# Sixteen narrow transfers for the MLP's two scalars, instead of 32 columns in the rows of its weights

## The chip, the cores and the metric

The kernel runs on one core of a Trainium2 chip, as one launch. The metric is device time in microseconds (us), the median over runs; lower is better. Profiles come from the hardware profiler and hold one execution each.

## The reference

One decoding step for 8 sequences: an attention block with grouped heads over a cache of 4096 keys, multiplied by the gate that a small gated MLP makes from the same normalised input. All is float32.

```python
xn = _layernorm(x)                                   # x: 8 x 1 x 512
# A: 32 query heads of 128, 8 key/value heads, caches 8 x 8 x 4096 x 128 (k and v)
q = (xn @ wq)                                        # wq: 512 x 4096
p = softmax(q k^T * 128**-0.5);  s = (p v) @ wo      # wo: 4096 x 512
# B: the MLP
z  = gelu(xn @ w_in)                                 # w_in: 512 x 1792
z1 = z[..., :896];  z2 = layernorm(z[..., 896:])
g  = w_sp * z2 + b_sp                                # w_sp is 1 x 1, b_sp has 1 element
B  = (z1 * g) @ w_out                                # w_out: 896 x 512
return x + s * silu(B)
```

The two scalars `w_sp` and `b_sp` are what this case is about.

## The kernel before

The caches and weights are rearranged on the host, so that each of the three large buffers in the core's memory (`slot_a`, `slot_b`, `slot_c`, each 128 partitions x 16384 floats, 8 MB) is filled by one transfer with one contiguous row per partition. All large transfers are issued by one engine's queue, SP's. The MLP's weights come as one array `w_mlp` of 128 rows: 7168 floats of `w_in`, 3584 of `w_out`, and 32 more, `side`, of which the first two are `w_sp` and `b_sp`, the same in each row. It goes into `slot_c`, which the first half of the first head's values takes over once the MLP is done.

Two parts follow each other.

- `prologue` is written against a scheduling library, which keeps the instructions of SP in the order of the code here and sets the semaphores itself. It has eight semaphores for transfers from SP's queue (named `DMAHW0` to `DMAHW7`) and hands them out in turn, one to each transfer. SP issues `wq` into `slot_b`, `x`, `w_mlp` into `slot_c`, and the first half of head 0's keys (`k0`, "in_kT") into `slot_a`; that one has a semaphore of its own, `landed_a`. Then come layer norm, the queries (L151, TensorE), their place in `q`, the second half of the keys (`k1`) into `slot_b` as soon as the queries are done (L161), and the MLP: products L176, GELU, layer norm, `z2 * w_sp + b_sp` at L202 on VectorE, products L211, and the gate at L224.
- `Heads` is ordered by hand, with semaphores of its own. For each of 8 heads: products with the two halves of the keys (L362), softmax, products with the two halves of the values (L384). `loads` issues on SP the transfers of 8 MB in the order in which buffers come free: values first half into `slot_c`, second half into `slot_b`, the next head's keys into `slot_a` and `slot_b`. `wo` comes in 7 pieces behind the last values. The first of these transfers, values into `slot_c` (L275), stands behind the end of the prologue on all engines.

At L202 the scalars are read from `side_sb`, the last 32 columns of the MLP's rows:

```python
nc.vector.tensor_scalar(z2, z2, side_sb[:, 0:1], side_sb[:, 1:2], op0=ALU.mult, op1=ALU.add)
```

Of the kernel before, what the change touches and what calls it, by code (L numbers as in the profile page):

```python
# [10 lines left out]
P = 128  # L11
B, D = 8, 512
# [4 lines left out]
R = 32  # L17
FH = 896
FQ = 256
NB = FH // P  # L20
# [9 lines left out]
AHEAD = FOLDED + 2  # L30
HD = 256
N_IN, N_OUT = NK * 2 * FH, NB * D
N_MLP = N_IN + N_OUT + R
STEPS = 8
WARM = 384
AHEAD_OF_V = 11
# [52 lines left out]
        self.same_all = self.same.rearrange("p g r -> p (g r)")  # L89


def prologue(tc, t, x, w_mlp, wq, k0, k1, landed_a, landed_b):

    nc = tc.nc
    slot_a, slot_b, slot_c = t.slots
# [1 line left out]
    wq_sb = slot_b.rearrange("p (k n) -> p k n", k=NK)  # L97
    w_in_sb = slot_c[:, :N_IN].rearrange("p (k n) -> p k n", k=NK)
    w_out_sb = slot_c[:, N_IN:N_IN + N_OUT].rearrange("p (j d) -> p j d", j=NB)
    side_sb = slot_c[:, N_IN + N_OUT:N_MLP]  # L100
    x_sb = slot_c[:B, N_MLP + P:N_MLP + P + D]
    xn = slot_c[:B, N_MLP + P + D:N_MLP + P + 2 * D]
    nc.sync.dma_start(x_sb, x)
    nc.sync.dma_start(slot_c[:, :N_MLP], w_mlp)
    first = nc.sync.dma_start(slot_a, k0).then_inc(landed_a, 16)
    tc.no_tile_sem_insts.add(first.ins.name)

# [341 lines left out]
        step(mm)  # L449


def gqa_gmlp_decode(nc, x, kT, v, wq, wo, w_mlp, x_rows, out):
    t = Chip(nc)
    landed_a, landed_b, stored = (nc.alloc_semaphore(s) for s in ("landed_a", "landed_b", "stored"))
    with tile.TileContext(nc) as tc:
        prologue(tc, t, x, w_mlp, wq, kT[0, 0], kT[0, 1], landed_a, landed_b)
    heads = Heads(nc, t, landed_a, landed_b, stored)
    heads.loads(kT, v, wo, x_rows)
    for h in range(HKV):
        heads.head_sides(h)  # L460
    heads.last_sides(out)
    nc.sync.wait_ge(stored, 16).then_inc(stored, -16)
    with nc.tensor.Fori(0, HKV):
        heads.head_products()
    heads.last_products()
# [39 lines left out]
```

## Time and profile before

| | |
|---|---|
| median of 3 runs | 678.76 us (678.47 to 679.23) |
| span of the profiled execution, first to last instruction | 677.3 us |
| that execution's place beside the runs | its span is 1.46 us below the median of the runs' device times |
| instructions | 5977 |
| busy: TensorE, VectorE, ScalarE, GpSimd | 409.4, 80.8, 13.8, 2.8 us |
| transfers | 290.90 MB in 6214 packets, 429 GB/s on average |

The profile numbers lines as the kernel above. A transfer's row gives the time at which SP starts to issue it; "us to landing" counts from there to the last of its completions. "SPq" is SP's queue of instructions; a share of DMA time is a share of what the core's 16 DMA engines could be busy.

### The profile page before, as it was taken

The numbers are of one execution on the slowest core, as the hardware profiler recorded it, in microseconds if no ns is written. First come the engines' busy times: TensorE is split into PE (matmuls) and PEld (weight loads), VectorE is DVE, ScalarE is ACT, GpSimd is POOL, SyncE is SP. The second block draws the span as 40 slices with busy tenths as digits, with TensorE's granted clock in tenths as the row PEclk, the third lists the DMA queues.
The fourth block names the chain that finished last, engine by engine and source line by source line (L and its number), as shares of the span: only waits on it lengthen the run. The fifth ranks groups of instructions, "written<-read, shape, count | busy, mean of one in ns | idle before, by whom it ended". The sixth has DMA issues, their size and how long they took to land. (4 is left out here: it accounts for less than half of the span.)

```text
span 677.3 us, 5977 instructions
## 1 busy us (share of the span) xinstructions
PE 409.4 (60%) x2660; PEld 134.0 (20%) x2660; DVE 80.8 (12%) x156; ACT 13.8 (2%) x28; POOL 2.8 (0%) x15
## 2 busy tenths in 40 slices
PE   0456749446875449455794459555693349655598
PEld 0112213112221113111131113111131113211134
DVE  0142021102110021101110021101100021100211
ACT  0010000000000000000000000000000000000000
POOL 1000000000000000000000000000000000000000
PEclk9986859787896669787696779877696788976699
DMA  9999999999999999999999999999999999999997
GB/s 379 443 433 434 434 434 433 434 433 433 433 433 433 433 433 433 433 433 433 433 433 433 433 433 433 433 433 433 433 433 433 433 433 434 433 433 433 433 448 300
DMA packets 6214, 290.90 MB, mean 429 GB/s; under 512 B 952, under 2 KB 1080, under 8 KB 1600
## 3 DMA queue, kind: packets, MB, share of 16 engines
q1 hardware_dynamic: 6064, 290.79, 99.3%
q8 instruction: 4, 0.07, 0.0%
q10 hardware_dynamic: 144, 0.03, 0.0%
q14 instruction: 2, 0.02, 0.0%
HBM read 290.78 MB, written 0.03 MB: 429 GB/s over the span
## 5 line engine op out<-in xcount | busy, mean ns | idle before, releaser
L362 PE MATMUL sc<-slot_b,q 128*32 128x512 f32 x512 | 73.8, 741 | 74.8 <-PEq L344 74.8
L362 PE MATMUL sc<-slot_a,q 128*32 128x512 f32 x512 | 72.9, 733 | 72.0 <-PEq L344 72.0
L384 PE MATMUL o_ps<-slot_c,pT 128*16 128x512 f32 x512 | 73.6, 739 | 48.4 <-PEq L344 48.4
L377 PE MATMUL scr<-pT,ident 128*128 128x512 f32 x176 | 77.7, 597 | 0.0
L384 PE MATMUL o_ps<-slot_b,pT 128*16 128x512 f32 x512 | 56.5, 593 | 4.2 <-PEq L344 4.2
L362 PEld LDWEIGHTS sc<-slot_b,q 128*32 128x32 f32 x512 | 20.7, 133 | 127.9 <-issue 127.9
L261 DVE TENSOR_REDUCE nm<-sc 128x1 f32<-128x1024 f32 x8 | 9.8, 1225 | 290.7 <-PE sc L362 290.7
L362 PEld LDWEIGHTS sc<-slot_a,q 128*32 128x32 f32 x512 | 20.1, 131 | 118.4 <-issue 118.4
L377 PEld LDWEIGHTS scr<-pT,ident 128*128 128x128 f32 x176 | 32.8, 190 | 45.1 <-issue 45.1
L261 DVE TENSOR_TENSOR o_all<-o_ps,diag 128x512 f32<-128x512 f32 x16 | 11.1, 692 | 225.2 <-PE o_ps L384 225.2
L384 PEld LDWEIGHTS o_ps<-slot_c,pT 128*16 128x16 f32 x512 | 17.3, 113 | 98.1 <-issue 98.1
L384 PEld LDWEIGHTS o_ps<-slot_b,pT 128*16 128x16 f32 x512 | 15.6, 97 | 44.2 <-issue 44.2
L292 ACT ACTIVATE p<-sc,nm 128x1024 f32<-128x1024 f32 x8 | 8.9, 1115 | 554.1 <-DVE nm L261 554.1
L261 DVE TENSOR_REDUCE o_sb<-o_all 128x128 f32<-128x512 f32 x16 | 16.5, 1033 | 0.5
L143 PE MATMUL scr<-ident,slot_c 8*128 8x8 f32 x4 | 0.6, 254 | 25.1 <-DVE slot_c L140 25.1
L349 PE MATMUL scr<-pT,ident 128*128 128x384 f32 x36 | 13.8, 507 | 0.0
L151 PE MATMUL scr<-slot_b,xnT 128*32 128x512 f32 x64 | 10.2, 792 | 0.3 <-DVE xnT L144 0.3
L261 DVE STREAM_TRANSPOSE pT<-p 128x1024 f32<-128x1024 f32 x8 | 10.0, 1245 | 0.3
L366 PE MATMUL scr<-ident,nm 128*1 128x128 f32 x8 | 2.2, 269 | 11.9 <-PEq L344 11.9
L370 PE MATMUL scr<-wl,same 128*128 128x1 f32 x16 | 3.6, 297 | 6.6 <-PEq L344 6.6
L392 PE MATMUL po<-fold,o_sb 128*128 128x16 f32 x32 | 6.1, 266 | 2.5 <-PEq L344 2.5
L392 PEld LDWEIGHTS po<-fold,o_sb 128*128 128x128 f32 x32 | 4.8, 188 | 14.0 <-issue 14.0
(94 smaller groups left out, 91.2 us busy)
## 6 DMA issues: line engine op xcount, KB each, us to landing
slot_c<-in_w_mlp SPq DMA_DIRECT2D x1, 5392.0 KB, 34.0
slot_a<-in_wo SPq DMA_DIRECT2D x1, 4608.0 KB, 39.1
slot_a<-in_wo SPq DMA_DIRECT2D x1, 1280.0 KB, 41.7
slot_a<-in_wo SPq DMA_DIRECT2D x2, 512.0 KB, 44.2
slot_a<-in_wo SPq DMA_DIRECT2D x1, 768.0 KB, 43.1
slot_a<-in_wo SPq DMA_DIRECT2D x1, 384.0 KB, 45.1
slot_a<-in_kT SPq DMA_DIRECT2D x8, 48.5
slot_b<-in_kT SPq DMA_DIRECT2D x8, 31.4
```

The source lines that it names most:

```text
L143: nc.tensor.transpose(pt[:, k * B:(k + 1) * B], xn[:, k * P:(k + 1) * P], t.ident[:B, :B])
L151: nc.tensor.matmul(pq[R * g:R * (g + 1), :], t.xnT[:, k, :], wq_sb[:, k, lo:lo + REP * DH], start=(k == 0), stop=(k == NK - 1))
L261: make(*args, **kw).then_inc(self.dve, 1)
L292: nc.scalar.activation(p, t.sc.rearrange("p c s -> p (c s)"), AF.Exp, bias=t.nm, accum_out=t.l).then_inc(self.act, 1)
L349: self.nc.tensor.matmul(t.scr[1][:, :WARM], t.ident, t.pT.rearrange("p j b g r -> p (j b g r)")[:, :WARM], start=True, stop=True)
L362: mm = nc.tensor.matmul(t.sc[R * g:R * (g + 1), c, :], t.q[:, b * R:(b + 1) * R], k_sb[:, i, c, g, :], start=(b == 0), stop=(b == B - 1))
L366: step(nc.tensor.transpose(t.scr[0][:1, :P], t.nm, t.ident))
L370: step(nc.tensor.matmul(t.scr[1][:, 1:2], t.same_all, t.wl, start=True, stop=True))
L377: nc.tensor.matmul(t.scr[1], t.ident, flat[:, :512], start=True, stop=True)
L384: mm = nc.tensor.matmul(of[R * i:R * i + G * REP, :], pT[:, j, half * HALF + i], v_sb[:, i, j], start=(j == 0), stop=(j == J - 1))
L392: mm = nc.tensor.matmul(t.po[:, half * n:(half + 1) * n], t.o_sb[half], t.fold.rearrange("p i r -> p (i r)"), start=True, stop=True)
```

## The change

The 32 columns leave `w_mlp`, whose rows become 10752 floats long instead of 10784. They come as an array of their own, `side` (128 rows of 32 floats, 128 bytes), into the same columns of `slot_c` as before, in sixteen transfers behind `w_mlp` on SP's queue: of 1, 2, 3 and so on up to 15 rows, and a last of 8 rows, 128 rows in all. The transfer of `k0` follows them.

```diff
-N_MLP = N_IN + N_OUT + R
+N_MLP = N_IN + N_OUT
...
-def prologue(tc, t, x, w_mlp, wq, k0, k1, landed_a, landed_b):
+def prologue(tc, t, x, w_mlp, side, wq, k0, k1, landed_a, landed_b):
...
-    side_sb = slot_c[:, N_IN + N_OUT:N_MLP]
+    side_sb = slot_c[:, N_MLP:N_MLP + R]
     x_sb = slot_c[:B, N_MLP + P:N_MLP + P + D]
     xn = slot_c[:B, N_MLP + P + D:N_MLP + P + 2 * D]
     nc.sync.dma_start(x_sb, x)
     nc.sync.dma_start(slot_c[:, :N_MLP], w_mlp)
+    row = 0
+    for rows in (*range(1, 16), B):
+        nc.sync.dma_start(side_sb[row:row + rows], side[row:row + rows])
+        row += rows
     first = nc.sync.dma_start(slot_a, k0).then_inc(landed_a, 16)
...
-            w_out.transpose(1, 0, 2).reshape(P, NB * D),
-            side], axis=1),
+            w_out.transpose(1, 0, 2).reshape(P, NB * D)], axis=1),
+        "side": side,
```

The lines of the changed kernel behind this place have numbers higher by 4 (L105 is L109, L202 is L206). On SP's queue, at the start of the program, stood before (the brackets name the semaphores on which a row waits):

```order
L96 DMA slot_b<-in_wq 128x16384
L103 DMA slot_c<-in_x 8x512
L104 DMA slot_c<-in_w_mlp 128x10784
L105 DMA slot_a<-in_kT 128x16384
L161 DMA slot_b<-in_kT 128x16384 [waits DMAHW0_52,PE_52]
```

In the changed kernel, behind `wq`, `x` and `w_mlp` and the transfers of 1 to 4 rows, none of which waits, there stands:

```order
L107 DMA slot_c<-in_side 5x32
L107 DMA slot_c<-in_side 6x32 [waits DMAHW0_52]
L107 DMA slot_c<-in_side 7x32 [waits DMAHW1_52]
L107 DMA slot_c<-in_side 8x32 [waits DMAHW2_52]
L107 DMA slot_c<-in_side 9x32 [waits DMAHW3_52]
L107 DMA slot_c<-in_side 10x32 [waits DMAHW4_52]
L107 DMA slot_c<-in_side 11x32 [waits DMAHW5_52]
L107 DMA slot_c<-in_side 12x32 [waits DMAHW6_52]
L107 DMA slot_c<-in_side 13x32 [waits DMAHW7_52]
L107 DMA slot_c<-in_side 14x32 [waits DMAHW0_52]
L107 DMA slot_c<-in_side 15x32 [waits DMAHW1_52]
L107 DMA slot_c<-in_side 8x32 [waits DMAHW2_52]
```

The transfer of `k0` (L109) stands behind the last of these rows, still without a wait of its own. The eight semaphores are handed out in turn, so that of `wq` is 0, of `x` 1, of `w_mlp` 2, of the sides of 1 to 5 rows 3 to 7; from the side of 6 rows on each transfer shares its semaphore with the one that stands eight places ahead of it in this row of transfers, and waits for that one's landing.

On VectorE, in the MLP, stood before:

```order
L191 TENSOR_SCALAR var<-scr 128x1 [waits PE_52]
L201 TENSOR_SCALAR p<-p,rs 128x256 [waits Pool_52]
L202 TENSOR_SCALAR p<-p,slot_c 128x256 [waits DMAHW2_52,DVE_52]
L203 TENSOR_TENSOR p<-p 128x256 [waits DVE_52]
L207 COPY pT<-scr 128x128 [waits PE_52] x2
```

and now:

```order
L195 TENSOR_SCALAR var<-scr 128x1 [waits PE_52]
L205 TENSOR_SCALAR p<-p,rs 128x256 [waits Pool_52]
L206 TENSOR_SCALAR p<-p,slot_c 128x256 [waits DMAHW4_52,DMAHW3_52,DMAHW5_52,DMAHW2_52,DMAHW6_52,DMAHW1_52,DMAHW7_52,DMAHW0_52,DVE_52]
L207 TENSOR_TENSOR p<-p 128x256 [waits DVE_52]
L211 COPY pT<-scr 128x128 [waits PE_52] x2
```

The order on VectorE is the same; the operation that reads the scalars waits for all eight transfer semaphores instead of one.

More of the change, by code (lines that the diff above doesn't have):

```diff
@@ L449, in last_products, with gqa_gmlp_decode @@
         step(mm)
-def gqa_gmlp_decode(nc, x, kT, v, wq, wo, w_mlp, x_rows, out):
+def gqa_gmlp_decode(nc, x, kT, v, wq, wo, w_mlp, side, x_rows, out):
     t = Chip(nc)
@@ L455, in gqa_gmlp_decode @@
     with tile.TileContext(nc) as tc:
-        prologue(tc, t, x, w_mlp, wq, kT[0, 0], kT[0, 1], landed_a, landed_b)
+        prologue(tc, t, x, w_mlp, side, wq, kT[0, 0], kT[0, 1], landed_a, landed_b)
     heads = Heads(nc, t, landed_a, landed_b, stored)
```

## The prediction

> **What bounds the kernel now.** I read the page first, its slices and queues, then busy time by stretches, then SP's own instructions in order of time. The page:
>
> ```profile
> span 677.3 us, 5977 instructions
> DMA  9999999999999999999999999999999999999997
> q1 hardware_dynamic: 6064, 290.79, 99.3%
> PE acc L428 0%; DVE gate L261 0%
> ```
>
> The 16 DMA engines are busy in each of the 40 slices but the last; SP's queue (q1) takes 99.3% of their time. The chain that ended last shows only the tail. TensorE, at 60%, is not the bound. By stretches:
>
> ```profile
> core 0: us, PE busy (x) PEld busy (x) DVE busy (x) ACT busy (x) POOL busy (x), PEclk, DMA share, GB/s
> 0.00:80.00 80.00, 34.77 (x236) 11.44 (x240) 15.32 (x41) 2.17 (x3) 2.83 (x15) 0.87 0.99 423
> 80.00:160.00 80.00, 50.11 (x310) 16.17 (x306) 8.10 (x14) 1.41 (x3) 0.00 (x0) 0.79 1.00 433
> 560.00:640.00 80.00, 51.12 (x310) 16.11 (x306) 7.90 (x13) 1.41 (x3) 0.00 (x0) 0.78 1.00 433
> ```
>
> From 80 to 640 us (the first and last of seven such stretches shown) the DMA share is 1.00, at 433 GB/s. So the time is bytes over rate, and any time in which the DMA engines have nothing queued is added to the end, because no later stretch has idle time to take it back. The question is whether the change leaves the engines without work. SP's issues in order of time:
>
> ```profile
> 0.74 0.37 SPq L96 DMA_DIRECT2D slot_b<-in_wq  x1
> 1.17 0.37 SPq L103 DMA_DIRECT2D slot_c<-in_x  x1
> 1.58 0.35 SPq L104 DMA_DIRECT2D slot_c<-in_w_mlp  x1
> 1.98 0.71 SPq L105 DMA_DIRECT2D slot_a<-in_kT  x1
> 37.59 0.33 SPq L161 DMA_DIRECT2D slot_b<-in_kT  x1
> 62.71 0.33 SPq L275 DMA_DIRECT2D slot_c<-in_v  x1
> 84.33 0.33 SPq L277 DMA_DIRECT2D slot_b<-in_v  x1
> 84.71 0.42 SPq L280 DMA_DIRECT2D slot_a<-in_kT  x1
> ```
>
> and from issue to landing (last column, us):
>
> ```profile
> slot_c<-in_w_mlp SPq DMA_DIRECT2D x1, 5392.0 KB, 34.0
> slot_b<-in_wq SPq DMA_DIRECT2D x1, 22.1
> slot_a<-in_kT SPq DMA_DIRECT2D x1, 52.9
> slot_b<-in_kT SPq DMA_DIRECT2D x1, 37.8
> slot_c<-in_v SPq DMA_DIRECT2D x1, 32.0
> ```
>
> Added to the issue times these give the landings: wq 22.84, w_mlp 35.58, k0 54.88, k1 75.39, the first values 94.71. Before, k0 is in the queue from 1.98 us on, 33.6 us before w_mlp has landed, so the engines go from the one to the other without a pause.
>
> **The change, part by part.**
>
> *Waits on SP.* In the new order SP issues wq, x, w_mlp and the sides of 1 to 5 rows without a wait, by about 4 us. The side of 6 rows waits for wq (semaphore 0) and that of 7 for x: both pass at 22.9 us, as the one wait for wq that before shows:
>
> ```profile
> L161 SPq EVENT_SEMAPHORE  x1: 17/17/17, 22.9 to 22.9; - x1
> ```
>
> That is 0.06 us behind the landing at 22.84, and costs nothing, since w_mlp is still moving. The side of 8 rows waits for semaphore 2, that of w_mlp: it can be issued at 35.58 + 0.06 = 35.64 us, and everything behind it on SP waits with it, k0 above all. By then the engines are empty but for a few rows of 128 bytes. The sides of 9 to 13 rows wait for those of 1 to 5, which lie in the queue right behind w_mlp and land with it; 14 and 15 wait for those of 6 and 7, the same. So nine issues stand between w_mlp's landing and k0's issue.
>
> *The price of one issue.* At the program's start issues follow each other by 0.43, 0.41 and 0.40 us (1.17 - 0.74 and so on); the shortest pair is 84.71 - 84.33 = 0.38; the longest run of issues is that of wo:
>
> ```profile
> 627.02 3.28 SPq L282 DMA_DIRECT2D slot_a<-in_wo  x7
> 630.34 16.94 SPq L283 DMA_DIRECT2D x_out<-in_x_rows  x1
> ```
>
> 7 in 630.34 - 627.02 = 3.32 us, 0.47 each. I take 0.41, the distance behind x, which is the nearest in kind (8 rows, under the library's semaphores): 9 x 0.41 = 3.7 us, bounds 3.4 and 4.3. A narrow transfer that takes as long to issue as the 0.71 of k0 would make 6.8 with 0.05 between; I keep that for the range. Below 0.38 no row goes. k0 is issued at 35.64 + 3.7 = 39.34 us instead of 1.98.
>
> *The last wait.* The last side (8 rows) shares semaphore 2 with the side of 8 rows at 35.64 and is reached eight issues later, at 38.9. The nearest landing of a small transfer on idle engines is the output's:
>
> ```profile
> out<-gate ACTq DMA_DIRECT2D x1, 32.0 KB, 1.5
> q10 hardware_dynamic: 144, 0.03, 6.2%
> ```
>
> 1.5 us from issue gives 37.1, so that wait is over 1.8 us before it is reached. It would bind only if a small landing took over 3.3 us.
>
> *The restart.* k0 is then the only work. wq is the one 8 MB transfer that starts on idle engines: 22.1 us from issue to landing. So k0 lands at 39.34 + 22.1 = 61.44 instead of 54.88: 6.56 us late. The lower bound: 8 MB in a running stream take 94.71 - 75.39 = 19.32 us (values behind k1), and a small transfer's 1.5 us covers issue, first packet and completion, in which its 144 packets take little: 19.3 + 1.4 = 20.7, 1.4 less. The upper: k0's own issue took 0.71, wq's 0.37, so 0.34 more. I take wq's, an identical transfer on an idle queue.
>
> *Extra packets.* 128 rows of data and their completions, some 256 packets more. The output's row prices a small packet: 6.2% of 16 engines over the 2.4 us of that answer, by 144, is 16.5 ns. 256 of them are 4.2 us of one engine, 0.26 us if spread. Here the most crowded engine may get one row and one completion of each transfer, 32 packets, 0.53 us. Those of 1 to 7 rows stand behind w_mlp and those of 8 and more in the pause, all ahead of k0's first packet. Covered by the pause; without it they would cost 0.26 to 0.53. By the Trainium skill ("DMA: Bandwidth & Descriptors", on why a DMA increments its semaphore by 16), a transfer uses the largest number of engines up to 16 that divides its rows, the lowest-numbered ones; the first engine then gets all sixteen. No view here splits the engines; this only chooses 0.53 over 0.26.
>
> *w_mlp shorter.* 128 x 128 bytes, 0.016 of 290.79 MB: 0.04 us at 433 GB/s, nothing.
>
> *What is queued behind k0.* k1's issue waits for the queries (37.59) and now also behind k0: 39.8, still 21 us ahead of k0's landing at 61.4. Covered. k1 lands near 82. L206 waits for all eight semaphores; the last side is issued at 38.9 and landed by 40.5, against the row
>
> ```profile
> L202 DVEq EVENT_SEMAPHORE  x1: 21/21/21, 52.9 to 52.9; - x1
> 53.26 0.41 DVE L202 TENSOR_SCALAR p<-p,slot_c 128x256 f32<-128x256 f32 x1
> 62.98 8.51 PE L362 MATMUL sc<-slot_a,q 128*32 128x512 f32 x64 [2.65 <-PEq L344]
> 75.51 4.91 PE L362 MATMUL sc<-slot_b,q 128*32 128x512 f32 x28 [4.01 <-PEq L344]
> ```
>
> 12 us early. Seven more waits of 0.02 us make 0.15 us, and as many again on SP at the prologue's end: the first values' issue moves from 62.71 to about 63.0, while k1 is moving until 82: covered by 19 us. TensorE's first products start at about 63.2, behind the 61.4 at which k0 has landed, and end 8.5 us later, before k1's 82. So TensorE waits longer for k1, and nothing of that shows. All later issues wait for TensorE's products of data that land 6.6 us later, and move with them.
>
> The 16.94 us of the last issue (L283) show that SP can be held in an issue when much is queued; there seven pieces of wo had gone out just before. In the new start eight transfers are out by 4 us and ten at 23 us; if that held SP too, it would hold it before w_mlp's landing, for which it has to wait anyhow.
>
> **The sum.** 3.7 (nine issues) + 0.06 + 22.1 - (54.88 - 35.58) = 6.56 us, 0 elsewhere. Against the profiled execution: span 677.3 + 6.6 = 683.9. The median of the runs stands 1.46 us above that span, and I add to it: 678.76 + 6.6 = 685.4 us, 1.0% slower.
>
> **Rivals.** *SP is not held (not slower).* If k0's issue came before about 34.1 us (w_mlp's landing at 35.58 less the output's 1.5), the queue would never run dry, and only the packets remain: 678.76 + 0.26 to 0.53 = 679.0 to 679.3, within 0.2%. For it: all issues take 0.4 us, 16 of them are 6.6 us, far ahead of 34.1. Against it: the order, in which the side of 8 rows waits for w_mlp's semaphore, and the row at 22.9, where SP did stand 20 us for such a semaphore. It decides at that one wait. 4%.
>
> *Each narrow transfer waits for the one before.* Then each of nine costs an issue and a landing, 0.37 + 1.5 = 1.9 us, 17.1 instead of 3.7: 6.6 + 13.4 = 20 us, 698.8. Against it: the waits name semaphores eight transfers back. 3%. The same page of the Trainium skill puts about 2.0 us of fixed cost on a DMA (section on the anatomy of one DMA, for transfers issued by GpSimd) and advises merging small ones; by that figure in turn the nine would be 18 us; the trace's 1.5 agrees in kind, but only if they were not in flight together.
>
> *Issuing narrow transfers is dear.* At 0.76 each the nine take 6.8 us: 9.7 us, 688.4. For it: issues of 3, 7 or 11 rows appear nowhere in this trace, and 0.71 does once. 10%.
>
> *The engines restart warm.* 20.7 instead of 22.1, and 0.38 an issue: 4.9 us, 683.6. 15%, the lower edge of the forecast's own spread.
>
> **The chances.** Forecast 67% (685.0 to 686.3 by the bounds of its issues, 3.4 and 4.3, and 0.34 on k0), the rivals 4, 3, 10 and 15%, and 1% for a gain of which I see no mechanism. The time is the forecast's. The range takes in the warm restart and the dear issues, 683.2 to 688.4, and leaves out about 1 in 10 (the first two rivals, and a little at both edges). Below 0.2% (1.36 us) a measurement of this kernel tells nothing from no change. Slower by more: 0.95; within: 0.04; faster: 0.01.
>
> **What would show it.** In SP's rows: an issue at L107 near 22.9 and one near 35.6, then nine at steps of about 0.4, L109 near 39.3 (before 1.98) with some 22 us to landing instead of 52.9. In the slices: the third (34.2 to 51.3 us of the longer span) falls from 433 to near 300 GB/s, all others stay; q1 has 6320 packets, and its share falls by about 0.8 points. L206 starts within 0.3 us of 53.3, the first values' issue within 0.5 of 62.7. Wrong would be: k0 issued before 34 us, steps of 0.7 or more, an idle stretch further on, or a later stage that takes some of the 6.6 us back.

## The result and the profile after

The changed kernel takes 684.67 us (684.52 to 684.86, 4 runs), against 678.66 us for the kernel before on the same chip: 1.0089 times as long, 95% interval 1.0077 to 1.0101. That is 6.0 us slower; 6.6 was forecast. The span of the profiled execution went from 677.3 to 683.2 us. Of the four runs of a kernel further down (`k0` ahead of the narrow transfers) one took 850.0 us; the numbers there are those of the other three.

The page of the changed kernel: span, slices of the DMA, and SP's queue.

```profile
span 683.2 us, 5998 instructions
DMA  9979999999999999999999999999999999999997
GB/s 399 415 308 427 430 427 434 435 430 430 430 430 445 453 437 430 430 434 430 430 434 437 430 430 430 430 460 441 434 430 430 434 430 430 437 434 430 430 438 304
q1 hardware_dynamic: 6320, 290.79, 98.5%
```

One slice fell, the third (34 to 51 us), to 308 GB/s. The busy digits of all others are those of before, so nothing was lost later and nothing made good. Of 16 engines' span SP's queue has 98.5% instead of 99.3. Around the hole, busy time by short stretches (the last two columns are the DMA share and GB/s):

```profile
33.00:35.00 2.00, 2.00 (x22) 0.68 (x24) 0.47 (x2) 0.00 (x0) 0.00 (x0) 1.00 0.57 238
35.00:36.00 1.00, 1.00 (x12) 0.26 (x8) 0.00 (x0) 0.00 (x0) 0.00 (x0) 1.00 0.00 0
36.00:38.00 2.00, 1.19 (x12) 0.42 (x4) 1.05 (x2) 0.00 (x0) 0.00 (x0) 1.00 0.03 3
38.00:40.00 2.00, 1.99 (x24) 0.76 (x26) 0.41 (x2) 0.00 (x0) 0.00 (x0) 1.00 0.43 134
```

From 35 to 38 us the DMA engines move 0 to 3 GB/s. SP's issues in order of time say why; the second answer begins at 35 us and so shows the last nine narrow transfers alone:

```profile
1.60 0.35 SPq L104 DMA_DIRECT2D slot_c<-in_w_mlp  x1
1.99 36.86 SPq L107 DMA_DIRECT2D slot_c<-in_side  x16
35.54 3.31 SPq L107 DMA_DIRECT2D slot_c<-in_side  x9
38.89 0.35 SPq L109 DMA_DIRECT2D slot_a<-in_kT  x1
39.28 0.43 SPq L165 DMA_DIRECT2D slot_b<-in_kT  x1
```

and the waits of SP's queue name what held it (total, times, longest, us):

```profile
SPq L107 <- DMA slot_b<-in_wq: 19.3, 1, 19.3
SPq L107 <- DMA slot_c<-in_w_mlp: 12.0, 1, 12.0
```

SP stood until 22.9 us for wq, which cost nothing, and until 35.54 for w_mlp. Then came nine issues in 3.35 us, and only then k0, at 38.89 us instead of 1.98. Time from issue to landing of k0 and k1:

```profile
DMA to landing us min/median/max: 23.1/23.1/23.1
DMA to landing us min/median/max: 42.0/42.0/42.0
```

k0 lands at 38.89 + 23.1 = 62.0 us (before 54.88) and k1 at 39.28 + 42.0 = 81.3 (before 75.39), 5.9 us late: the loss of the whole kernel is complete by then.

### The profile page after: what moved, and what is told of

It is laid out like the page before. It is cut to its first block, busy times and chain, and to the rows that moved or that the text cites. A ratio compares the mean times of both kernels' runs of the same rounds, so it can differ in the third digit from the quotient of the medians.

```text
span 683.2 us, 5998 instructions
## 1 busy us (share of the span) xinstructions
PE 408.5 (60%) x2660; PEld 133.3 (20%) x2660; DVE 80.8 (12%) x156; ACT 13.8 (2%) x28; POOL 2.8 (0%) x15
## 3 DMA queue, kind: packets, MB, share of 16 engines
q1 hardware_dynamic: 6320, 290.79, 98.5%
```

## The experiments

Three accounts were set against each other. *The held queue*: the transfers share eight semaphores, so that SP waits for w_mlp's landing ahead of k0's issue, and the engines run empty. *The small packets*: the 256 packets more cost the time. *Issues ahead of k0*: sixteen issues stand ahead of it, whatever they wait for.

**Seven and eight transfers.**

```diff
-    for rows in (*range(1, 16), B):
+    for rows in (1, 2, 3, 4, 3, 3, 112):       # seven
+    for rows in (1, 2, 3, 3, 2, 2, 3, 112):    # eight, in another kernel
```

For seven was expected:

> The 128 rows in seven transfers on SP's queue, of 1, 2, 3, 4, 3, 3 and 112 rows: the last still has a wait, but for x, none for w_mlp. If SP's wait for w_mlp's landing makes the loss (the held queue): k0 is issued at about 23.6 us, w_mlp is still moving until 35, no pause, 678.7 to 679.0 us. If the small packets make it (256 of them for 6.0 us): 160 packets here, +3.8, 682.4. If it is only that issues stand ahead of k0, whatever they wait for (sixteen for 6.0 us): seven, +2.6, 681.3.

For eight:

> The same rows in eight transfers, of 1, 2, 3, 3, 2, 2, 3 and 112 rows; 160 packets as with seven. The held queue: the eighth waits for w_mlp's landing, SP goes on at 35.5 and issues k0 after one transfer, at 35.95 instead of the 38.89 of the changed kernel, 2.9 us less loss: 681.7 us, 3.0 above seven transfers, with a pause of some 2 us in the DMA. The small packets: 682.4, the same as seven. Issues ahead of k0 alone: 0.4 above seven.

Measured: seven 678.49 us, a ratio of 0.9999 (0.9990 to 1.0009) to the kernel before; eight 681.62, 1.0045 (1.0028 to 1.0062). One transfer more, with the same number of packets, costs 3.1 us. SP's issues with seven:

```profile
1.97 21.46 SPq L107 DMA_DIRECT2D slot_c<-in_side  x7
23.48 0.43 SPq L109 DMA_DIRECT2D slot_a<-in_kT  x1
```

and with eight (from 35 us on):

```profile
35.48 0.32 SPq L107 DMA_DIRECT2D slot_c<-in_side  x1
35.84 0.44 SPq L109 DMA_DIRECT2D slot_a<-in_kT  x1
```

and from its waits:

```profile
SPq L107 <- DMA slot_c<-in_w_mlp: 12.1, 1, 12.1
```

With seven, SP is held as well, until 22.8 us and for wq; k0 is issued 12 us before w_mlp has landed, and nothing is lost. With eight the last transfer takes w_mlp's semaphore, k0 comes at 35.84, and the engines run empty. Packets alone and issues alone are out: neither can make a step of 3 us between seven and eight.

**Thirty-two transfers of 4 rows.** `for rows in (4,) * 32:`

> The change with 32 transfers of 4 rows: 25 of them stand between w_mlp's landing and k0's issue, instead of 9. The held queue, at the 0.27 us that the issue of 4 rows took in the changed kernel and 0.04 between: 25 x 0.31 = 7.7 us, k0 at 43.2 us, 4.3 later than in the changed kernel, 689.0 us. At the prediction's 0.41 an issue: 10.3 us, 691.6. The small packets: 256 of them as in the change, 684.7.

Measured: 689.49 us, 1.0163 (1.0146 to 1.0180). From 35 us on:

```profile
35.37 8.36 SPq L107 DMA_DIRECT2D slot_c<-in_side  x25
43.77 0.35 SPq L109 DMA_DIRECT2D slot_a<-in_kT  x1
```

25 issues in 8.4 us, 0.336 each; k0 at 43.77. The loss follows the issues that stand behind the wait.

**k0 ahead of the narrow transfers.**

```diff
+    first = nc.sync.dma_start(slot_a, k0).then_inc(landed_a, 16)
+    tc.no_tile_sem_insts.add(first.ins.name)
     row = 0
     for rows in (*range(1, 16), B):
...
-    first = nc.sync.dma_start(slot_a, k0).then_inc(landed_a, 16)
-    tc.no_tile_sem_insts.add(first.ins.name)
```

> k0 is issued ahead of the sixteen transfers, at 1.98 us as before the change. The held queue: the pause does not go but moves. The sides of 1 to 5 rows now land behind k0 (54.5 us), the side of 9 rows waits for that of 1, and k1 stands behind eight more issues, 3.0 us, at about 57.5 instead of 37.6; the DMA is empty from 54.5 on. The loss is the changed kernel's 6.0 less one issue of 0.32: 684.3 us. Issues ahead of k0 alone: 678.7. The small packets: 684.7, with no pause.

Measured: 684.16 us, 1.0083 (1.0063 to 1.0103): hardly better than the change itself. SP's issues from 54 us on:

```profile
54.50 2.97 SPq L109 DMA_DIRECT2D slot_c<-in_side  x8
57.52 0.35 SPq L165 DMA_DIRECT2D slot_b<-in_kT  x1
```

and from its waits:

```profile
SPq L109 <- DMA slot_c<-in_side: 18.9, 1, 18.9
```

The pause moved one transfer further: the sides now land behind k0, and k1 is the one that stands behind them, issued at 57.52 instead of 37.59.

**What a pause costs.** Four kernels have a pause behind a wait of SP's; the delay is the issue of the next 8 MB less the moment at which SP goes on:

| | SP goes on | next 8 MB issued | delay | loss against before | rest |
|---|---|---|---|---|---|
| eight transfers | 35.48 | 35.84 | 0.36 | 3.07 | 2.71 |
| k0 first | 54.50 | 57.52 | 3.02 | 5.61 | 2.59 |
| the change | 35.54 | 38.89 | 3.35 | 6.01 | 2.66 |
| thirty-two | 35.37 | 43.77 | 8.40 | 10.97 | 2.57 |

The loss is the delay plus 2.6 to 2.7 us, over a range of 0.4 to 8.4 us. So once the queue is left to run dry, it costs 2.6 us before a single extra issue is counted. The trace's packet records show what these are in the changed kernel. The first 64 KB packets of k0, one on each engine, start at 34.76 us on average in the kernel before. SP goes on only at 35.54, 0.78 later; the packets start 1.20 us behind k0's issue, at 40.09; and they take 3.12 us on average instead of 2.42, as those of wq at the program's start do (3.11). 0.78 + 1.20 + 0.70 = 2.68 us.

**The same sixteen from ScalarE's queue.** `nc.scalar.dma_start(...)` in place of `nc.sync.dma_start(...)` for the narrow transfers.

> The sixteen transfers as in the change, with the same waits, but issued by ScalarE's queue, so that SP's has only wq, x, w_mlp and k0. The held queue: ScalarE is held until w_mlp lands and nobody waits for it before 45 us; k0 is issued in the first 5 us; 678.7 to 679.3 us. The small packets: 256 of them still, 684.7. Issues ahead of k0 alone: 678.7.

Measured: 682.91 us, 1.0065 (1.0048 to 1.0082). The expectation was wrong. SP's issues:

```profile
0.74 0.37 SPq L96 DMA_DIRECT2D slot_b<-in_wq  x1
24.01 0.35 SPq L103 DMA_DIRECT2D slot_c<-in_x  x1
24.42 0.35 SPq L104 DMA_DIRECT2D slot_c<-in_w_mlp  x1
24.81 0.43 SPq L109 DMA_DIRECT2D slot_a<-in_kT  x1
```

From its waits:

```profile
SPq L103 <- DMA slot_c<-in_side: 22.9, 1, 22.9
```

and from busy time by stretches (share and GB/s of the DMA at the end):

```profile
20.00:23.00 3.00, 0.00 (x0) 0.00 (x0) 0.00 (x0) 0.00 (x0) 0.00 (x0) 1.00 0.01 1
```

The eight semaphores serve both queues. The library put ScalarE's transfers ahead of x in the turn, so that x got the semaphore of the side of 9 rows, which itself stood behind the wait for wq on ScalarE. SP was held from 1.1 to 24.0 us, and the DMA moved 1 GB/s from 20 to 23 us: the pause had moved ahead of w_mlp. It is the same mechanism at a third place. By the table's account, ScalarE goes on at 22.70 us, the next large transfer, w_mlp, is issued at 24.42, and the loss of 4.36 less this delay of 1.72 leaves 2.64, as in the other four. But the narrow transfers behind the wait again lie in the pause, so this run doesn't tell packets from waits, for which it was made.

**Sixteen transfers on a semaphore of their own.** The kernel before, with the scalars in the MLP's rows as ever, and the sixteen transfers added to the queue; their data goes to a spare 128 bytes per partition:

```diff
     nc.sync.dma_start(slot_c[:, :N_MLP], w_mlp)
+    row = 0
+    for rows in (*range(1, 16), B):
+        part = nc.sync.dma_start(t.spare[row:row + rows], side[row:row + rows]).then_inc(landed_side, 16)
+        tc.no_tile_sem_insts.add(part.ins.name)
+        row += rows
...
+    nc.vector.wait_ge(landed_side, 256).then_inc(landed_side, -256)
     heads.loads(kT, v, wo, x_rows)
```

> The kernel before, scalars in the MLP's rows as ever, with the sixteen transfers of 1 to 15 and 8 rows added behind w_mlp on SP's queue, into 128 bytes per partition that nobody reads; they count on one semaphore of their own, so that none of them waits. The held queue: SP issues all sixteen by 7 us and k0 then; no pause; 678.6 us, up to 0.7 more if the most crowded of the DMA engines (32 packets of some 22 ns) is the last one. The small packets: 256 of them, 684.6. Issues ahead of k0 alone: sixteen, 684.6.

Measured: 680.12 us, 1.0023 (1.0013 to 1.0033). SP's issues, none of which at L108 had to wait:

```profile
1.99 5.62 SPq L108 DMA_DIRECT2D spare<-in_side  x16
7.65 0.35 SPq L111 DMA_DIRECT2D slot_a<-in_kT  x1
```

Without the wait 4.4 of the 6.0 us are gone, and k0 is issued at 7.65 us. But 1.6 remain, more than the 0 to 0.7 expected. (Its 22 ns are what the records below give for a row and its completion together, not for each of 32 packets.) The slices of DMA rate from 53 to 57 us, where k1 follows k0 (0.1 us each, packets counted where they start), of the kernel before:

```profile
GB/s 0 0 0 0 0 0 0 0 0 3932 2622 1311 1966 0 0 655 0 0 0 0 0 0 0 0 0 0 0 0 0 0 0 0 0 3932 2621 655 2621 0 0 655
```

and of this one:

```profile
GB/s 0 655 0 0 655 655 1311 0 0 0 1311 1966 0 1311 655 0 0 0 0 0 0 655 655 655 0 0 655 0 0 1311 1311 0 0 0 1311 1966 0 1311 655 0
```

Before, all 16 engines go over to k1 within 0.7 us (53.9 to 54.6). Now they straggle over two microseconds. The trace's packet records show where it starts: the first 64 KB packet of k0 takes 2.42 us on every engine before, and here 2.42 to 4.37, while the narrow packets themselves are recorded at 13 ns and their completions at 9. The engines are late behind the narrow transfers, not in them.

**One row each, and the same number on all engines.** The same kernel with `(1,) * 16` and with `(16,) * 8` rows (the semaphore then counts to 128).

> As the kernel with sixteen added transfers on a semaphore of their own, but each of 1 row: 16 rows and, on the most crowded engine, the same 16 transfers. If the 1.6 us of that kernel are those of the one most crowded DMA engine, which takes part in all sixteen: 680.1 us again, and one engine late by 2 us behind k0. If they go by packets: 32 of 256, +0.2, 678.7. If they go by SP's issues (16 each): 680.1, with no engine late.

> The same with eight transfers of 16 rows: 128 rows and 128 completions, 256 packets as with 1 to 15 and 8 rows, but the same on each engine, 8 transfers each instead of up to 16. The most crowded engine: half of 1.6 us, 679.3 us, with the engines as close together behind k0 as in the kernel before. By packets: 680.1. By SP's issues: half, 679.3.

Measured: one row each 678.96 us, 1.0005 (0.9995 to 1.0014); eight of 16 rows 679.18, 1.0006 (0.9997 to 1.0016), near the 679.3 expected. In the packet records one row each leaves exactly one engine late: its first packet of k0 takes 4.38 us, the other fifteen 2.42. Eight of 16 rows leave all sixteen late by 0.3 to 0.8 us (2.72 to 3.20). So it goes by what one engine gets: some 2 us for sixteen transfers, half a microsecond or a little more for eight. In all three kernels a transfer brings each of its engines one row and one completion, so these runs don't tell an engine's transfers from its packets. Packets in total are out: eight transfers of 16 rows have the 256 of the first kernel and cost 0.5 us instead of 1.6, though for one row each that account's 678.7 came near. SP's issues are out by one row each, with sixteen of them and 680.1 expected. Both intervals take in 1: that most of the 1.6 us is gone is shown, that 0.3 and 0.5 us are left is not. On the engines' choice the Trainium skill ("DMA: Bandwidth & Descriptors", on why a DMA increments its semaphore by 16) has a transfer of one row on one engine, the lowest-numbered; that one engine alone is late agrees, though no view here gives an engine's number.

The time was expected wrongly all the same, 680.1 for one row each. One engine late by 2 us cost some 0.3 us at the end, it seems because others end late anyway: the last 64 KB packets end between 653.15 and 654.90 us in the kernel before, and between 652.89 and 655.17 with one row each, the last 0.3 us behind the former last; which engine that is the records don't say. With 1 to 15 and 8 rows nine engines were late by 0.2 to 2 us, and the last packet ended at 656.52. That the delays that engines get later fall upon engines that were late already is my reading; no run tells it apart.

## Why the prediction was right

- *The bound.* Right: no stage after the pause took anything back. The loss is 5.9 us at k1's landing and 6.0 at the end. The row of 16.94 us, where SP was held in an issue, has no counterpart at the start: with sixteen narrow transfers behind wq, x and w_mlp, all issued by 7.6 us, k0's issue took 0.35 us.
- *The wait.* Right, by eight against seven transfers (3.1 us) and by the queue with a semaphore of its own. Its place was right too: the side of 8 rows at 35.54 us (35.64 forecast).
- *Nine issues.* 3.35 us measured, 3.7 forecast: the price of 0.41, from x, was too high by a tenth. The lower bound was misread: the trace before has pairs of issues 0.37 us apart (121.26 and 121.63), not only 0.38, and of the nine measured steps, 0.31 to 0.42 us, the shortest lies below both. This is the larger part of the 0.6 us between forecast and result; with the 0.1 at the resumption, k0 came 0.45 us earlier than forecast.
- *The restart.* The sum had 0.06 + 22.1 - 19.30 = 2.86 us for it; the table shows 2.57 to 2.71. The cold start was the right row, the warm one (20.7 in place of 22.1, so 1.5) was not. k0's own row, 23.1, is not a clean price: a packet of instructions went through the DMA while it moved,

```profile
q8 instruction: 4, 0.07, 0.0%
```

  one of the four of each profile, 0.96 us long in the packet records, at 57.7 us; in the kernel before it came at 59.0 and fell upon k1. With thirty-two transfers it came at 40.0 us, in the pause, and k0 landed 21.8 us after its issue, near the 22.1 of wq; with eight it fell upon k0 again, which took 23.1.
- *The last wait.* Right: SP's last narrow issues follow each other without a stop up to 38.89 us.
- *Extra packets.* Their place was right, covered by the pause, so that they add nothing to the sum. Their size was wrong: 0.26 to 0.53 us was forecast for the case without a pause, 1.6 was measured there. The recorded length of small packets misses what they do to the packet behind them.
- *Covered work.* L206 starts at 52.45 us (53.26 before) and the first values are issued at 61.69 (62.71): the MLP was not held at all. The prediction had these up to 0.3 us later; they came up to 1.0 earlier, and nothing depends on it.
- *Rivals.* "SP is not held" fell with the row at 35.54, "each waits for the one before" with nine issues in 3.35 us. "Dear issues" fell for narrow ones.

## What to carry to other kernels

Where a queue keeps the DMA full, count the semaphores that its transfers share: the transfer that takes one over waits for the landing of the one before it, and everything behind it in the queue waits with it, though nobody needs its data yet. The question is not how many bytes or issues are added, but whether the queue holds enough work at that moment: seven transfers were free here, and the eighth cost 3 us. Moving the large transfer ahead only moves the pause to the next one; fewer transfers, or a semaphore of their own, take it away (of the sixteen of uneven rows 1.6 us stayed even so).

## What the runs showed of the hardware that was not expected

- An issue's price on SP goes with the rows of narrow transfers, from 1 to 16: sixteen of 1 row took 4.77 us, 0.30 each, and eight of 16 rows 3.87, 0.48 each. It doesn't go on like that: the transfer of 112 rows took 0.36 (35.48 to 35.84), wq and w_mlp with 128 rows 0.43 and 0.40 in the kernel before. SP's issues with one row each:

```profile
1.99 4.73 SPq L108 DMA_DIRECT2D spare<-in_side  x16
6.76 0.35 SPq L111 DMA_DIRECT2D slot_a<-in_kT  x1
```

and with 16 rows each:

```profile
1.98 3.83 SPq L108 DMA_DIRECT2D spare<-in_side  x8
5.85 0.43 SPq L111 DMA_DIRECT2D slot_a<-in_kT  x1
```

- Narrow transfers between large ones make the next large packet of the engines that they use late, by up to 1.96 us behind sixteen of them (4.38 against 2.42), though their own packets are recorded at 13 and 9 ns.
- A DMA queue that ran dry cost 2.6 to 2.7 us more than the delay itself, in all five kernels with such a pause. In the changed kernel SP went on 0.78 us after the engines would have gone over to k0, k0's first packets started 1.20 us behind its issue, and they took 0.70 us longer than in a running stream.
